# Which engine waits for the last store: SyncE's final semaphore wait placed on ScalarE

## The chip, the cores and the metric

One core of a Trainium2 chip. The metric is the device time of one execution in microseconds (us), median over the runs; every run also leaves its span, from its first to its last profiled instruction of the kernel. The device time is longer than the span, here by 1.4 us, and that difference is what this study is about. Where the timed interval starts no trace shows; where its end is placed among the trace's events below, it is counted from the span's start. All runs quoted are of the fast state. The one exception among the listed times is the first run of the kernel before, 324.55 us, which enters no comparison.

## The reference, cut to what matters

One decoding step: attention of one token over a window of 4096 cached keys (32 query heads, 16 key heads), and beside it a GELU layer, mixed by a gate. The result is a single row of 576 bfloat16 numbers.

```python
g = _sigmoid((x * gate_w).sum(-1, keepdims=True))
a = _A_ref(x, A_k_cache, A_v_cache, A_wq, A_wo)   # attention over the last 4096 positions
b = _B_ref(x, B_w1, B_b1, B_w2, B_b2)             # 576 -> 4608 -> 576 with GELU
return g * a + (1 - g) * b
```

Some 54 MB of cache and weights are read (53.62 MB by the page), 1152 bytes are written (one packet of the trace).

## The kernel before

The body ends with two casts of the accumulated row, one half on ScalarE and one on VectorE, and the store from SyncE's queue:

```python
    out_row = const.tile([1, D], BF16, name="out_row")
    nc.scalar.copy(out=out_row[:, DH:D], in_=y_out[1])
    nc.vector.tensor_copy(out=out_row[:, 0:DH], in_=y_out[0])
    nc.sync.dma_start(out=out.rearrange("a b d -> (a b) d"), in_=out_row[:])
```

When the program is complete, a function rewrites its closing block. Instead of one barrier that all engines pass, SyncE gets six event semaphores. Each waits until one semaphore has its final count and takes that count away again; the sixth is the store's own. GpSimd clears the other semaphores as two ranges as soon as ScalarE, TensorE and VectorE have drained (in the trace the last of the three drains, VectorE's, ends at 128.934 us, and the two clears run from 129.143 to 129.336).

```python
        sem = store.sync_info.on_update[0].id
        act = mybir.EngineType.Activation
        names = [i.name for i in end.instructions if i.engine == sp]
        names += [i.name for i in end.instructions if i.engine == act][1:]
        # ... mine: the waits on ScalarE's, VectorE's, two load queues' and TensorE's
        # ... semaphores, and last the store's
        for w, name in zip(mine, names):
            taken = mybir.SyncUpdate(..., update_mode="sem-sub-imm", update_value=w.wait_value)
            kept.append(copy.replace(leave, name=name,          # leave: an instruction of SyncE
                sync_info=mybir.SyncInfo(on_wait=[w], on_update=[taken])))
        for engine in (Activation, PE, DVE):                    # (cut) their drains
            kept.append(next(i for i in end.instructions if i.engine == engine))
        # ... GpSimd: wait for the three drains, two range clears
```

Of the kernel before, what the change touches and what calls it, by code (L numbers as in the profile page):

```python
# [18 lines left out]
def kernel(  # L19
# [91 lines left out]
    def store_ends_program(nc):  # L111
        body, end = nc.main_func.blocks[1], nc.main_func.blocks[2]
        sp, pool = mybir.EngineType.SP, mybir.EngineType.Pool
        store = [
            i
            for i in body.instructions
            if i.engine == sp and type(i).__name__ == "InstDMACopy"
        ][-1]
        sem = store.sync_info.on_update[0].id
        act = mybir.EngineType.Activation  # L120
        names = [i.name for i in end.instructions if i.engine == sp]
        names += [i.name for i in end.instructions if i.engine == act][1:]
        drain, arrive, leave = [i for i in end.instructions if i.engine == sp][:3]
        waits = list(drain.sync_info.on_wait)
        pe = [
            u
            for i in body.instructions
            if i.engine == mybir.EngineType.PE and i.sync_info
            for u in i.sync_info.on_update
        ]  # L130
        first = min(w.id for w in store.sync_info.on_wait)
        mine = [w for w in waits if w.id >= first and w.id != sem]
        mine.append(
            copy.replace(
                mine[0],
                id=pe[0].id,
                ant_name=pe[0].ant_name,
                wait_value=sum(u.update_value for u in pe),
            )
        )  # L140
        mine.append(next(w for w in waits if w.id == sem))
        stop = max(w.id for w in mine) + 1
        assert sorted(w.id for w in mine) == list(range(first, stop))
        waits = [w for w in waits if w.id < first]
        own = [i for i in body.instructions if i.engine == sp and i.sync_info]
        last_wait = max(
            n for n, i in enumerate(own) if any(w.id < first for w in i.sync_info.on_wait)
        )
        last_load = max(
            n for n, i in enumerate(own) if any(u.id < first for u in i.sync_info.on_update)  # L150
        )
        assert last_wait <= last_load
        assert len(names) >= len(mine)
        kept = []
        for w, name in zip(mine, names):
            taken = mybir.SyncUpdate(
                sync_type="semaphore",
                id=w.id,
                ant_name=w.ant_name,
                update_mode="sem-sub-imm",  # L160
                update_value=w.wait_value,
                update_reg=None,
            )
            kept.append(
                copy.replace(
                    leave,
                    name=name,
                    sync_info=mybir.SyncInfo(on_wait=[w], on_update=[taken]),
                )
            )  # L170
        for engine in (
            mybir.EngineType.Activation,
            mybir.EngineType.PE,
            mybir.EngineType.DVE,
        ):
            kept.append(next(i for i in end.instructions if i.engine == engine))
        ours = [i for i in end.instructions if i.engine == pool]
        others = mybir.SyncInfo(on_wait=waits, on_update=[])
        came = ours[1].sync_info
        three = mybir.SyncInfo(  # L180
            on_wait=[copy.replace(came.on_wait[0], wait_value=3)],
            on_update=[copy.replace(came.on_update[0], update_value=3)],
        )
        kept += [copy.replace(ours[0], sync_info=others), copy.replace(ours[1], sync_info=three)]
        reset, clear, spare, spare2 = ours[3:7]
        lo, hi = reset.reset_range_start, reset.reset_range_stop
        for n, (a, b) in enumerate(((lo, first), (stop, hi))):
            raw = list(clear.instr)
            assert raw[13:15] == [lo, hi - 1]
            raw[13:15] = [a, b - 1]  # L190
            words = dict(clear.ant_dict, range_first=a, range_last=b - 1)
            kept.append(
                copy.replace(
                    reset, name=(reset, spare)[n].name, reset_range_start=a, reset_range_stop=b
                )
            )
            kept.append(
                copy.replace(
                    clear, name=(clear, spare2)[n].name, instr=raw, ant_dict=words
                )  # L200
            )
        end.instructions = kept

    nc.at_finalize(store_ends_program)

    const = ctx.enter_context(tc.tile_pool(name="const", bufs=1))
# [561 lines left out]
```

## Time and profile before

| | kernel before |
|---|---|
| device time, three runs | 131.5, 131.64 us (and the 324.55 of the first run) |
| span of the profiled run, its device time | 130.1 us, 131.53 us |
| VectorE's last cast ends | 128.887 us |
| the store is issued, lands | 128.956, 130.079 us |
| SyncE's wait for it ends | 130.113 us |

Read it backwards from the end: the time beyond 130.11 is no instruction of the kernel, and between 129.24 and 130.08 no engine does anything that counts; one of them waits for the store. The prediction below shows the lines of the page on which this rests.

### The profile page before, as it was taken

The page shows a single profiled execution, that of the slowest core. Times are in us where ns is not written, and L with a number is a line of the kernel's source. Part 1 is how long each engine was busy: PE and PEld are TensorE (multiplying, and loading weights), DVE is VectorE, ACT ScalarE, POOL GpSimd, SP SyncE. Part 2 cuts the span into 40 slices and gives each one's busy share as a digit, 9 for nine tenths or more (in the row PEclk, how much of TensorE's full clock was granted, in tenths as well). Part 3 has the DMA queues.
Part 4 walks back from the last instruction along what each step waited for, and adds up shares of the span by engine and source line. Part 5 has one row for each costly group of instructions (what it writes and reads, how often), then busy time and mean ns, then how long its engine had stood idle before and what let it go on. Part 6 is the DMA issues. An engine that isn't in the chain of part 4 may idle for free.

```text
span 130.1 us, 2403 instructions
## 1 busy us (share of the span) xinstructions
PE 79.7 (61%) x1148; PEld 45.6 (35%) x1077; DVE 52.3 (40%) x48; ACT 8.3 (6%) x18; POOL 9.2 (7%) x26
## 2 busy tenths in 40 slices
PE   0037999476003998939918994995300830899573
PEld 0037679375000121201211120595300830855441
DVE  0153000400079959999999995614000020010001
ACT  2000000003000000030003003011000000000001
POOL 7039700000000000000000000000000000000000
PEclk9999999999999999999997799985555555559999
DMA  6999999799899999999899899899899899999980
GB/s 232 427 431 432 476 424 476 344 484 448 373 458 453 403 433 463 393 433 484 373 433 484 383 423 484 357 432 505 368 433 489 363 438 415 442 401 427 413 363 33
DMA packets 2508, 53.75 MB, mean 413 GB/s; under 512 B 286, under 2 KB 290, under 8 KB 580
## 3 DMA queue, kind: packets, MB, share of 16 engines
q1 hardware_dynamic: 2490, 53.61, 96.5%
q8 instruction: 8, 0.13, 0.4%
q10 hardware_dynamic: 10, 0.01, 0.0%
HBM read 53.62 MB, written 0.00 MB: 412 GB/s over the span
## 4 chain that ended last, share of the span: by engine, by line
DMA 52%; DVE 24%; PE 14%; issue 6%; SPq 2%
DMA k_t<-in_A_k_cache_dram 27%; DMA w_t<-in_B_w_dram 25%; DVE kt L531 19%; PE s_ps L553 7%; PE o_ps L640 5%; DVE m L569 3%; DVE pt L602 2%; PE y_ps L396 1%; SPq L684 1%; DVE mr L572 1%; SPq L691 0%; DVE out_row L736 0%; SPq L234 0%; SPq L230 0%; PE mt_ps L578 0%
## 5 line engine op out<-in xcount | busy, mean ns | idle before, releaser
L553 PE MATMUL s_ps<-kt,qz_flat 128*128 128x512 bf16 x128 | 32.9, 414 | 17.2 <-DVE kt L531 10.4
L531 DVE STREAM_TRANSPOSE kt<-k_t 128x4096 f32<-128x4096 f32 x8 | 35.3, 4433 | 12.2 <-DMA k_t<-in_A_k_cache_dram 10.5
L640 PE MATMUL o_ps<-pt,v_t 128*128 128x8 bf16 x512 | 14.2, 168 | 16.6 <-DMA v_t<-in_A_v_cache_dram 14.7
L553 PEld LDWEIGHTS <-qz_flat 128*128 128x128 bf16 x64 | 6.9, 107 | 40.6 <-issue 40.4
L640 PEld LDWEIGHTS <-v_t 128*128 128x128 bf16 x512 | 14.0, 102 | 17.3 <-DMA v_t<-in_A_v_cache_dram 14.9
L424 PEld LDWEIGHTS <-w_t 128*128 128x128 bf16 x162 | 10.3, 167 | 1.8 <-issue 1.8
L424 PE MATMUL h_ps<-x,w_t 128*128 128x2 bf16 x162 | 10.5, 202 | 0.0
L590 ACT ACTIVATE p_t<-s_ps,negm 128x1024 bf16<-128x1024 f32 x4 | 4.5, 1114 | 50.9 <-DVE negm L586 50.9
L396 PE MATMUL y_ps<-w_t,gt 128*1 128x288 bf16 x72 | 6.3, 329 | 1.2 <-DMA w_t<-in_B_w_dram 1.2
L670 DVE RECIPROCAL rg<-mt_ps 128x32 f32<-128x32 f32 x1 | 0.4, 358 | 15.6 <-PE mt_ps L665 15.6
L602 DVE STREAM_TRANSPOSE pt<-p_t 128x1024 bf16<-128x1024 bf16 x4 | 4.9, 1225 | 2.7 <-ACT p_t L590 2.7
L462 PE MATMUL q_ps<-x,wq_t 128*128 128x2 bf16 x144 | 4.0, 166 | 2.9 <-DMA wq_t<-in_A_wq_dram 2.9
L569 DVE TENSOR_REDUCE m<-s_ps 128x1 f32<-128x1024 f32 x4 | 4.8, 1196 | 1.1 <-PE s_ps L553 1.1
L396 PE MATMUL y_ps<-wo_t,ov 128*1 128x288 bf16 x62 | 4.3, 285 | 1.4 <-DMA wo_t<-in_A_wo_dram 1.4
L736 DVE CAST out_row<-y_ps 1x288 bf16<-1x288 f32 x1 | 0.4, 445 | 11.6 <-PE y_ps L396 11.6
L433 DVE COPY hacc<-h_ps 128x36 f32<-128x36 f32 x1 | 0.2, 196 | 11.9 <-PE h_ps L424 11.9
L462 PEld LDWEIGHTS <-wq_t 128*128 128x128 bf16 x144 | 3.9, 104 | 3.0 <-DMA wq_t<-in_A_wq_dram 3.0
L345 PE MATMUL xs_ps<-one_b,rows 1*128 1x1 bf16 x9 | 0.7, 196 | 6.9 <-DVE rows L339 6.9
L396 PEld LDWEIGHTS <-gt 128*1 128x1 bf16 x72 | 3.3, 92 | 3.4 <-issue 1.6
L694 DVE TENSOR_TENSOR om<-o_ps,rgh 128x128 bf16<-128x128 f32 x1 | 0.3, 291 | 8.6 <-PE o_ps L640 8.6
L396 PEld LDWEIGHTS <-ov 128*1 128x1 bf16 x62 | 2.6, 83 | 2.8 <-issue 1.9
L339 DVE COPY rows<-rows 1x1152 bf16<-1x1152 bf16 x1 | 0.7, 748 | 6.1 <-DMA rows<-in_A_x_dram 6.1
(72 smaller groups left out, 35.5 us busy)
## 6 DMA issues: line engine op xcount, KB each, us to landing
k_t<-in_A_k_cache_dram SPq DMA_DIRECT2D x4, 4096.0 KB, 32.1
v_t<-in_A_v_cache_dram SPq DMA_DIRECT2D x4, 4096.0 KB, 22.8
wq_t<-in_A_wq_dram SPq DMA_DIRECT2D x1, 4608.0 KB, 25.8
w_t<-in_B_w_dram SPq DMA_DIRECT2D x1, 2880.0 KB, 14.1
w_t<-in_B_w_dram SPq DMA_DIRECT2D x1, 2592.0 KB, 22.9
w_t<-in_B_w_dram SPq DMA_DIRECT2D x1, 2304.0 KB, 8.1
wo_t<-in_A_wo_dram SPq DMA_DIRECT2D x1, 2304.0 KB
wo_t<-in_A_wo_dram SPq DMA_DIRECT2D x1, 2160.0 KB
```

Source lines behind the costliest of these rows:

```text
L339: nc.vector.tensor_copy(out=xdup.rearrange("p (d t) -> p d t", t=2), in_=x_row.rearrange("p (d o) -> p d o", o=1).to_broadcast([1, D, 2]),)
L396: last = nc.tensor.matmul(y_out[s], lhsT=vec, rhs=row[:, s * DH : (s + 1) * DH], start=start, stop=stop, skip_group_check=True,)
L424: nc.tensor.matmul(h_ps[:, j:NF:NJ], lhsT=w1_t[:, i, j:FH:NJ], rhs=x2[:, i, :], start=False, stop=(i == NI - 1 and j == NJ - 1), skip_grou ...
L462: nc.tensor.matmul(q_ps[:, j : Hq : Hq // 2], lhsT=wq_t[:, i, j * Dh : (j + 1) * Dh], rhs=x2[:, i, :], start=(i == 0 and j == 0), stop=(i ...
L531: lambda: nc.vector.transpose(out=kt[g, f][:].bitcast(FP32), in_=keys.rearrange("p c d -> p (c d)").bitcast(FP32),),
L553: last = nc.tensor.matmul(s_ps[g][:, u * 512 : (u + 1) * 512].rearrange("p (c k) -> p c k", k=32), lhsT=qz(g, j, 2 * f + half), rhs=kv[:, ...
L569: queue("dve", lambda: nc.vector.reduce_max(out=m1[:], in_=s_ps[g][:], axis=AX.X))
L572: lambda: nc.vector.tensor_scalar(out=mr[:], in0=hi16[:], scalar1=m1[:, 0:1], scalar2=None, op0=ALU.mult),
L590: nc.scalar.activation(out=p_t[:].rearrange("p c k -> p (c k)"), in_=s_ps[g][:], func=ACT.Exp, bias=negm[:, 0:1], scale=SCALE, accum_out=s ...
L602: lambda: nc.vector.transpose(out=pt[:, g, :, :].rearrange("p c q -> p (c q)"), in_=p_t[:].rearrange("p c k -> p (c k)"),),
L640: last = nc.tensor.matmul(o_ps[:, 8 * g : 8 * g + 8, 0], lhsT=v_t[g][:, c, :], rhs=pt[:, g, c % 32, 8 * (c // 32) : 8 * (c // 32) + 8], st ...
L684: nc.sync.dma_start(out=wo_t[:, r0:r1, :].rearrange("p r n -> p (r n)"), in_=wo_src[:, 0 : 4 * RW, :].rearrange("h (a r) n -> h a (r n)", ...
```

## The change

The store's wait is moved from SyncE, which issued the store, to ScalarE, which has nothing else to do then (its last instruction, the drain, ends at 128.903). The intent is that SyncE gets through its five other take-backs and is finished early, and that an idle engine takes over the wait. The arithmetic, the loads and the store stay as they are. The two lines on `names` only lend the sixth take-back a spare name; it is taken off the list again (`kept.pop()`), and what it waits for goes to ScalarE's own closing instruction.

```diff
-        act = mybir.EngineType.Activation
         names = [i.name for i in end.instructions if i.engine == sp]
-        names += [i.name for i in end.instructions if i.engine == act][1:]
+        names.append([i.name for i in end.instructions if i.engine == pool][-1])
@@
+        landing = kept.pop().sync_info
         for engine in (Activation, PE, DVE):                    # (cut)
             kept.append(next(i for i in end.instructions if i.engine == engine))
+        event = [i for i in end.instructions if i.engine == mybir.EngineType.Activation][1]
+        kept.append(copy.replace(event, sync_info=landing))
```

## The prediction

Where the recorded text said more of the machine than a trace or a run of this case shows, it is cut, and the cut is marked. No term of its sum is among the cuts: 131.64 + 0.174 + 0.022 = 131.84 us if ScalarE is second in the order, 131.75 if it is fourth. Some of its words, in terms of the trace: a round, or the barrier, is nine updates of semaphore 2 in a row; "forward" are its first five updates, "the way back" its last four, "the turn" is the time from the fifth to the sixth; "the reset" are the writes to the semaphores 7 to 255 that the trace shows from 130.37 to 130.97. The records used here give an update's semaphore and its time and not its engine. The order of the engines is therefore the author's inference from when each one's last instruction ends, and e0 to e3 test it. That nothing afterwards absorbs the difference (step 5) is the author's estimate.

> **What bounds the kernel now.** I read the page from the front: the span, the slices, the chain that ended last; then the end of the program, because that is all that the change touches.
>
> ```profile
> span 130.1 us, 2403 instructions
> DMA  6999999799899999999899899899899899999980
> q1 hardware_dynamic: 2490, 53.61, 96.5%
> DMA 52%; DVE 24%; PE 14%; issue 6%; SPq 2%
> ```
>
> The transfers are busy in every slice but the last, and the queue of loads has 96.5% of the 16 engines' time. 53.6 MB have to be read, so loading is the bound, up to about 128 us. Nothing of that is in the diff: no load, no tile, no wait of the body changes. The chain in order of time shows what is left after the last load:
>
> ```profile
> 94.29 32.93 DMA w_t<-in_B_w_dram
> 127.22 0.04 issue
> 127.27 1.19 PE y_ps L396 x16
> 128.45 0.43 DVE out_row L736
> ```
>
> The last rows of w2 land at 127.2, sixteen matmuls and one cast follow, and the chain stops at 128.88. The timeline of the last two microseconds goes on:
>
> ```profile
> 128.44 0.45 DVE L736 CAST out_row<-y_ps 1x288 bf16<-1x288 f32 x1 [11.62 <-PE y_ps L396]
> 128.48 0.39 ACT L735 CAST out_row<-y_ps 1x288 bf16<-1x288 f32 x1 [11.47 <-PE y_ps L396]
> 128.96 0.28 SPq L737 DMA_DIRECT2D out_dram<-out_row  x1
> ```
>
> SyncE issues the store at 128.96. From there to the end of the span, 130.11, the page shows no busy engine. The view of the closing line of the program says what stands there:
>
> ```profile
> L763 SPq EVENT_SEMAPHORE  x6: 17/17/17, 129.3 to 130.1; - x6
> L763 POOLq EVENT_SEMAPHORE  x4: 17/30/43, 116.7 to 129.0; - x4
> L763 POOLq EVENT_SEMAPHORE_RANGE_CLEAR  x2: 33/52/71, 129.1 to 129.3; - x2
> L763 PEldq DRAIN  x1: 497/497/497, 128.0 to 128.0; - x1
> L763 ACTq DRAIN  x1: 421/421/421, 128.5 to 128.5; - x1
> ```
>
> SyncE's six semaphore instructions are what the diff is about: each waits for one semaphore and takes it back to zero. The columns give only count, duration and first and last start. The trace's own records, which the views merge, give each one (us from the span's start; semaphore 110 is the store's):
>
> ```
> SyncE event semaphores start   129.289 129.376 129.449 129.528 129.595 | 130.096 (on 110, ends 130.113)
> updates of semaphore 110       129.394   130.079   130.113
> last instruction ends          TensorE 128.525, ScalarE 128.903, VectorE 128.934, GpSimd 129.336
> updates of semaphore 2, after  128.731 129.062 129.863 129.907 130.250 | 130.294 130.333 130.367 130.413
> updates of semaphore 2, before -0.378 -0.344 -0.306 -0.262 -0.239 | -0.126 -0.088 -0.054 -0.007
> updates of semaphore 2, last   131.198 131.232 131.270 131.462 131.485 | 131.583 131.621 131.655 131.702
> ```
>
> Two things are to be seen. First, SyncE has done its five other take-backs at 129.61 and then stands until the store lands at 130.079; it wakes 17 ns later, and that is the last instruction of the span. Second, the program's end isn't the end of the time: 131.53 us were timed for this execution, 1.42 more than the span. No semaphore of the kernel is number 2; it goes up nine times in a row just before the first instruction, nine times after the last, and nine more times a microsecond later. Between the last two rows some 250 semaphores are written in five runs of numbers (7 to 53, 54 to 104, 105 to 155, 156 to 206, 207 to 255) from 130.37 to 130.97. So what follows the kernel waits for all engines, and the question of this change is only how late, and from which engine, that barrier is closed.
>
> [...] The trace shows these two updates of semaphore 110, at 129.394 and 130.079; only the second matters, whoever waits. [...]
>
> [...] Read the row "after". At 130.250 the fifth update comes, 137 ns after SyncE's last instruction. The four before it came at 129.907 or earlier, when SyncE still stood in its wait. So SyncE is fifth[...]. The first, at 128.731, can only be TensorE's, as all others were still in the program. The second, 129.062, is 159 ns after ScalarE's end (or 128 after VectorE's). The third, 129.863, comes after GpSimd's end at 129.336, and the fourth follows it by only 44 ns, so it belongs to an engine that was already waiting. I take the order TensorE, ScalarE, GpSimd, VectorE, SyncE. The trace leaves one alternative, ScalarE and VectorE exchanged.
>
> **The change part by part.** Removed from SyncE: its sixth event semaphore, which waited for 110. Added to ScalarE: the same instruction after its drain. Unchanged: the store, its landing, the five other take-backs, GpSimd's two range clears.
>
> 1. SyncE's five take-backs end at 129.61 before and after. They weren't on the path (0.47 us ahead of the landing), so SyncE gains nothing that counts: it goes into the barrier about 129.75 and stands there.
> 2. ScalarE ends its drain at 128.90, over a microsecond before the landing, so it is waiting at 130.079 as SyncE was. I give it the same 17 ns to wake and 17 to execute: 130.113. The span stays at 130.1.
> 3. From its last instruction to its barrier update ScalarE took 159 ns against SyncE's 137: plus 22 ns. ScalarE's update comes at about 130.272.
> 4. Before, when SyncE was the late one, the four others had already gone forward: only the way back was left, 130.250 to 130.413, or 163 ns. Now ScalarE is late, second in the row: GpSimd, VectorE and SyncE have still to go forward[...]. The round before the kernel has just that shape, as all came close together: second to ninth update, -0.344 to -0.007, 337 ns. It contains a turn of 113 ns (-0.239 to -0.126), where after the kernel the turn took 44[...].
> 5. Difference: 337 - 163 = 174, plus 22 of step 3, so about 0.20 us. It is the same at the sixth update[...]: 218 - 44 = 174. So nothing afterwards absorbs it.
>
> Sum: 131.64 + 0.20 = 131.84 us if ScalarE is second. If it is fourth, what remains is fourth to ninth, -0.262 to -0.007, 255 ns against 163: 92 + 22, so 0.11 us and 131.75. I weigh the first at four to one and say 131.8.
>
> **The rivals.** Rival one: the intent works and the end comes sooner, because SyncE is freed early and ScalarE answers faster. For it: SyncE is the last engine of the program. Against it: it is last only because of the landing, which waits for the DMA alone, 1.12 us from the start of its issue. The wake was 17 ns, so there is nothing to be saved there; even an instant one gives 131.62. Rival two: nothing at all, because the timed interval stops before the barrier or because the reset work of an engine released early hides it. For it: I can't see where the timed interval starts and stops. Against it: 1.42 us lie outside the span, about what the barrier and the reset take[...]. It would make 131.64. Rival three: ScalarE does something more before the barrier than its 159 ns, as GpSimd does (129.336 to 129.863, 0.53 us). Then plus 0.5: 132.1 to 132.2. Against it: ScalarE's own 159 ns in the same trace. Rival four: the instructions reach ScalarE late, or the loads shift. There is no sign of it; the body keeps its order.
>
> **Range and chances.** All rivals lie between 131.6 and 132.2; two quiet runs before were 131.5 and 131.64, so noise of 0.15 is added below. Range 131.5 to 132.2. Two per cent is 2.6 us, more than the whole stretch from the store's issue to the span's end (1.15 us) and more than any rival: within 2% at 97 in 100. The rest is for a different chip state, a little more on the slow side, since the granted clock fell to five tenths in nine slices of before.
>
> **What would show it.** Right: the span stays within 0.2 us of 130.1 with its last event semaphore on ScalarE some 17 ns after the store's landing; SyncE's list has five instead of six and ends near 129.6; semaphore 2 has only one update (TensorE's) ahead of that moment, then eight in a chain of about 0.34 us. Step 4 is wrong if three or four updates are already there (ScalarE then stands late in the order), step 3 if ScalarE's update comes much later than 0.16 us after its last instruction, and step 5 if the chain is longer and the time isn't. The whole prediction falls if the landing itself moves by more than 0.3 us against the store's issue, or if the time changes in the body, ahead of 128.

## The result, and the profile after

| | before | changed |
|---|---|---|
| median of the first comparison | 131.63 us (4 runs) | 131.84 us (131.66 to 132.01, 4 runs) |
| ratio, 95% interval | | 1.0019 [0.9999, 1.0039] |
| span of the profiled run | 130.1 us | 130.3 us |
| device time less span, profiled run | 1.42 us | 1.59 us |

A ratio is the mean time of one kernel's fast runs over that of the other's of the same rounds, so not quite the ratio of the medians quoted. The interval touches 1, so from these runs' times alone one couldn't say that anything happened. The trace says it.

The page's first lines of the changed kernel, with the queue of loads as busy as before:

```profile
span 130.3 us, 2403 instructions
q1 hardware_dynamic: 2490, 53.61, 96.4%
```

The closing line of the program in the changed kernel (the columns are count, shortest, median and longest duration in ns, first and last start):

```profile
L765 SPq EVENT_SEMAPHORE  x5: 17/17/17, 129.4 to 129.8; - x5
L765 POOLq EVENT_SEMAPHORE  x4: 17/30/43, 116.8 to 129.1; - x4
L765 POOLq EVENT_SEMAPHORE_RANGE_CLEAR  x2: 33/52/71, 129.3 to 129.5; - x2
L765 ACTq DRAIN  x1: 419/419/419, 128.6 to 128.6; - x1
L765 ACTq EVENT_SEMAPHORE  x1: 17/17/17, 130.3 to 130.3; - x1
```

SyncE has five instead of six and is done at 129.8. The sixth stands on ScalarE, 1.2 us after its drain, and starts at 130.3 as SyncE's started at 130.1. Where the 0.2 us between these two come from, the timeline of the end shows:

```profile
128.61 0.45 DVE L738 CAST out_row<-y_ps 1x288 bf16<-1x288 f32 x1 [11.65 <-PE y_ps L398]
128.64 0.39 ACT L737 CAST out_row<-y_ps 1x288 bf16<-1x288 f32 x1 [11.49 <-PE y_ps L398]
129.12 0.28 SPq L739 DMA_DIRECT2D out_dram<-out_row  x1
```

The casts start 0.16 us later in this run than in the one of before (128.44 there), and the store likewise. That lies ahead of everything that was changed, and the chain in order of time puts it with the loads, whose last rows land at 127.39 in place of 127.22:

```profile
127.39 0.04 issue
127.43 1.19 PE y_ps L398 x16
128.62 0.43 DVE out_row L738
```

It is a difference of these two runs and not of the kernels: over all runs the spans' median is 130.25 us for the changed kernel here and 130.30 in a later set, and 130.3 to 130.4 for the kernel before in three later sets. What is left is after the store. The trace's records, in us from the span's start:

```
                                         before                            changed
store lands (semaphore 110)              130.079                           130.243
event semaphore on 110, end              130.113 (SyncE)                   130.281 (ScalarE)
semaphore 2, first round after           128.731 129.062 129.863 129.907   128.895
                                         130.250                           130.430 130.469 130.513 130.536
                                         130.294 130.333 130.367 130.413   130.634 130.672 130.706 130.753
landing to ninth update                  0.334                             0.510
last round, fourth and ninth update      131.462 131.702                   131.799 132.040
device time                              131.53                            131.87
```

Before, four updates were there when the landing came, and five followed it. In the changed kernel only TensorE's is there, and eight follow in a chain of 0.32 us. From the landing on, the changed kernel takes 0.176 us more up to the ninth update, and 0.174 more up to the last one of the last round (1.797 against 1.623). The device time ends 0.17 us ahead of that last update in both. So the two profiled runs' 0.34 us are 0.164 up to the landing, by chance, and 0.176 in the barrier after it.

### The profile page after: what moved, and what is told of

It is laid out like the page before. It is cut to its first block, busy times and chain, and to the rows that moved or that the text cites. A ratio compares the mean times of both kernels' runs of the same rounds, so it can differ in the third digit from the quotient of the medians.

```text
span 130.3 us, 2403 instructions
## 1 busy us (share of the span) xinstructions
PE 80.8 (62%) x1148; PEld 45.7 (35%) x1077; DVE 52.3 (40%) x48; ACT 8.3 (6%) x18; POOL 9.2 (7%) x26
## 3 DMA queue, kind: packets, MB, share of 16 engines
q1 hardware_dynamic: 2490, 53.61, 96.4%
## 4 chain that ended last, share of the span: by engine, by line
DMA 50%; DVE 24%; PE 15%; issue 6%; SPq 3%
DMA k_t<-in_A_k_cache_dram 27%; DMA w_t<-in_B_w_dram 23%; DVE kt L533 19%; PE s_ps L555 9%; PE o_ps L642 5%; DVE m L571 3%; DVE pt L604 2%; SPq L686 2%; PE y_ps L398 1%; DVE mr L574 1%; SPq L693 0%; SPq L236 0%; DVE out_row L738 0%; SPq L232 0%; PE mt_ps L580 0%
## 5 line engine op out<-in xcount | busy, mean ns | idle before, releaser
L398 PE MATMUL y_ps<-w_t,gt 128*1 128x288 bf16 x72 | 6.9, 343 | 1.2 <-DMA w_t<-in_B_w_dram 1.2
```

Source lines behind the costliest of these rows:

```text
L398: last = nc.tensor.matmul(y_out[s], lhsT=vec, rhs=row[:, s * DH : (s + 1) * DH], start=start, stop=stop, skip_group_check=True,)
```

## The experiments

As in the prediction, "the barrier" is the round of nine updates of semaphore 2; the "place theory" is the prediction's account, that each engine's first update has a fixed place in that round and that the cost is set by the place of the late engine, which e0 to e3 test; "landing to ninth" is the time from the store's landing to the ninth update of the first round after the kernel. "Outside the span" is the device time less the span, median over the runs of a set. For the kernel before it is 1.44, 1.43 and 1.41 us in three sets (11, 11 and 9 runs), steadier than the device time, in which the body's 0.1 to 0.2 us are contained. Three calls were made; the four kernels of each ran on one chip against shared runs of the kernel before.

### First call: the wait on each of the other engines

**e0, ScalarE again.** The changed kernel, no edit, more rounds.

> The changed kernel as it is, with more rounds, since one set of four runs left the interval at 0.9999 to 1.0039. Place theory[...]: +0.18 us against before, ratio about 1.0014, and in the trace 0.51 us from the store's landing to the ninth update of semaphore 2 (before 0.33). Rival, the body: the 0.16 us that the changed kernel's profile showed ahead of the store is real; then +0.35 us, ratio 1.0027, with the store issued 0.16 us later than before again. Rival, nothing: 1.0000.

Measured: ratio 1.0015 [0.9999, 1.0032], 131.93 against 131.70 us. Landing to ninth 0.510 us again; outside the span 1.64 us against 1.44. The profiled run's store is issued late again, at 129.185 against 128.956, as the rival "body" expected; but the spans have the same median, 130.3, and the profiled runs of e6 and e7, which have the body of the kernel before, issue it at 129.224 and 129.065. So that rival is out. The size agrees with the place theory; the interval of the times still touches 1, and the evidence is the trace and the time outside the span: all ten runs of the changed kernel have 1.56 to 1.65 us there, 29 of the 31 of the kernel before 1.39 to 1.48.

**e1, VectorE.**

```diff
-        event = [i for i in end.instructions if i.engine == mybir.EngineType.Activation][1]
+        event = [i for i in end.instructions if i.engine == mybir.EngineType.DVE][1]
```

> The landing wait on VectorE. Place theory with the order TensorE, ScalarE, GpSimd, VectorE, SyncE: VectorE's update is the fourth, after three that are there already; fourth to ninth takes 0.25 us as before the kernel, so landing to ninth is about 0.43 us if VectorE needs as long as ScalarE from its last instruction to its update (0.15), +0.10 us, ratio 1.0008. If VectorE and ScalarE were exchanged in the order, its update is second and the cost +0.18. Rival, ScalarE itself answers slowly or does more at its end and the place is irrelevant: as before, 0.33 us, ratio 1.0000.

Measured: ratio 1.0020 [1.0001, 1.0039], landing to ninth 0.485 us. Three updates are there before the landing (128.834, 129.162, 129.958), and VectorE's is the fourth, 130.424. So VectorE is fourth, ScalarE second, and the one alternative that the prediction left open is excluded. Fourth to ninth took 0.240 us (expected 0.25). VectorE needed 0.196 us from its last instruction to its update, more than the 0.15 assumed. The time outside the span, 1.77 us, is 0.2 more than this chain makes of it; see e10.

**e2, TensorE.** The same edit with `PE`.

> The landing wait on TensorE. Place theory: TensorE is first, so no update of semaphore 2 comes before its own, and the whole round of nine follows, 0.36 us; TensorE took 0.245 us from its last instruction to its update. Landing to ninth 0.64 to 0.68 us, +0.30 to +0.35 us against before, ratio 1.0023 to 1.0027; the largest but for GpSimd. Rival, ScalarE alone is slow: as before. Rival, any engine but SyncE costs the same: +0.18.

Measured: ratio 1.0030 [1.0012, 1.0049]. No update comes before 130.752, then nine in 0.357 us. Landing to ninth 0.705 us, a little over the expected 0.68, of which 0.269 are TensorE's way from its last instruction to its update (0.245 expected) and 0.051 the event semaphore itself, which takes 17 ns on the others and 21 on VectorE:

```profile
L765 SPq EVENT_SEMAPHORE  x5: 17/17/17, 129.6 to 129.9; - x5
L765 PEldq EVENT_SEMAPHORE  x1: 51/51/51, 130.4 to 130.4; - x1
```

In this view of e2's closing line SyncE is again done half a microsecond ahead of the landing, which is at 130.404. Outside the span are 1.72 us against 1.44, and 0.045 more lie inside it, as the event semaphore ends 79 ns after the landing instead of 34: together some 0.33 of the trace's 0.371.

**e3, GpSimd.** The wait comes after its range clears.

```diff
-        event = [i for i in end.instructions if i.engine == mybir.EngineType.Activation][1]
-        kept.append(copy.replace(event, sync_info=landing))
@@ after the range clears
+        kept.append(copy.replace(ours[1], name=ours[-1].name, sync_info=landing))
```

> The landing wait on GpSimd, after its two range clears. Place theory: GpSimd is third, two updates are there, third to ninth takes about 0.29 us. GpSimd took 0.53 us from its last instruction to its update before; [...]landing to ninth is 0.85 us, +0.52 us against before, ratio 1.0040. If the 0.53 us are the range clear still at work, which the landing then hides, it is 0.17 us instead and the cost +0.15 us. Rival, ScalarE alone is slow: as before.

Measured: ratio 1.0051 [1.0027, 1.0075]; landing to ninth 0.882 us, two updates ahead of the landing; outside the span 2.00 us against 1.44, so 0.56 more where the trace has 0.548. From GpSimd's last instruction to its update 0.557 us pass, though the last range clear had ended 0.79 us before that instruction did. So this half microsecond isn't the clears at work; what GpSimd does in it no record shows.

The four late engines and SyncE side by side (us, from the traces; the way home is from the late engine's update to the ninth):

| late engine | place | updates ahead of the landing | last instruction to its update | way home | landing to ninth |
|---|---|---|---|---|---|
| SyncE (before) | 5 | 4 | 0.137 | 0.163 | 0.334 |
| VectorE (e1) | 4 | 3 | 0.196 | 0.240 | 0.485 |
| GpSimd (e3) | 3 | 2 | 0.557 | 0.284 | 0.882 |
| ScalarE (e0) | 2 | 1 | 0.150 | 0.322 | 0.510 |
| TensorE (e2) | 1 | 0 | 0.269 | 0.357 | 0.705 |

The way home grows with each place towards the front, step by step by 77, 44, 38 and 35 ns. The rival "ScalarE alone is slow" would have left e1, e2 and e3 at 0.33 us. ScalarE's own way out is next to the shortest.

### Second call: no landing to wait for, and a different store

**e4 and e5, an early store.** Their outputs are wrong, which doesn't matter for the times. Both store a row that VectorE makes early, e4 in the kernel before and e5 in the changed one. The lowest semaphore of the take-backs is then named by VectorE's, as the store no longer waits for it.

```diff
+    b2_early = const.tile([1, D], BF16, name="b2_early")
+    nc.vector.tensor_copy(out=b2_early[:], in_=b2g[:])
@@
-        first = min(w.id for w in store.sync_info.on_wait)
+        first = min(w.id for w in waits if w.ant_name.startswith('DVE'))
@@
-    nc.sync.dma_start(out=out.rearrange("a b d -> (a b) d"), in_=out_row[:])
+    nc.sync.dma_start(out=out.rearrange("a b d -> (a b) d"), in_=b2_early[:])
```

> Wrong result on purpose: the kernel before, but the store carries a row that VectorE makes early (the scaled b2), so it lands before the last cast ends and the landing wait on SyncE is met at once. Place theory: the late engine of the barrier is then GpSimd (0.53 us after its last instruction), third in the order; third to ninth takes 0.28 us. Ninth update about 1.26 us after VectorE's last cast ends, where before it was 1.53: the time falls by some 0.27 us, ratio 0.998. Rival, the time is set by something else than the landing: no change.

> Wrong result on purpose: the changed kernel with the same early store. Place theory: a wait that ends early costs nothing wherever it stands, because GpSimd is late in both, so this agrees with e4_early_syncE within 0.02 us in the trace (cast end to ninth update 1.26 us) and within noise in time. Rival, the instruction on ScalarE, or ScalarE's end of program, costs the 0.18 us by itself: then this is 0.18 us slower than e4_early_syncE and close to before.

Measured: the store is issued at 101.74 and 101.96 us, among the loads, and lands at 128.29 and 128.09, ahead of the last cast's end (129.10 and 129.13). Cast end to ninth update is 1.253 and 1.252 us, as expected (1.26), and equal in the two. But the times hardly fell: ratios 0.9996 [0.9979, 1.0012] and 0.9999 [0.9987, 1.0011] where 0.998 was expected. The barrier gained its 0.27 us and the end lost most of them: in e5's trace the cast's end to the end of the device time is 2.562 us against 2.643 before. (e4's profiled run, 132.16 us, is the slowest of its set and lost more, 3.057.) What the traces show there: in both, a packet of 8192 bytes appears at 131.46 and 131.48 us, on the queue that also brings packets of that size before the kernel starts (six of them, from -11.32 to -8.60 us, in the trace of before, where they are of the kind "instruction"), lasting 0.995 and 0.493 us; the writes to the semaphores 156 to 206, called VectorE's resets here because e10 moves them, start at 130.79 and 130.82 in place of 130.43, although the ninth update came earlier (130.35 and 130.38, by the cast's end and the time after it, against 130.413); and the device time follows the end of that packet, less 0.29 us, in both. The kernel before and the changed one have no such packet. e1 has one, at 131.757. Common to e1, e4 and e5 is one instruction more on VectorE: 59 recorded in the trace, 58 in the kernel before and in the changed one. I took the packet for instructions of VectorE, which was a guess (the expectations call the packet a fetch, and the guess the fetch theory).

**e6 and e7, the store in pieces.** The kernel before, the store described as 2 by 288 (e6) and 16 by 36 (e7).

```diff
-    nc.sync.dma_start(out=out.rearrange("a b d -> (a b) d"), in_=out_row[:])
+    nc.sync.dma_start(out=out.rearrange("a b (h d) -> (a b) h d", h=2), in_=out_row[:].rearrange("p (h d) -> p h d", h=2))
```

> The kernel before (wait on SyncE) with the store described as 2 pieces of 288 in place of one of 576, to see whether the landing can come sooner. I have no firm number: 1.12 us from issue to landing as before, give or take 0.1. Place theory: whatever is gained at the landing is gained at the ninth update one for one, up to the 0.27 us at which GpSimd becomes the late engine; what is lost is lost in full.

> The same with 16 pieces of 36. [...] Issue to landing 1.0 to 1.3 us; the ninth update follows the landing by 0.33 us as before, as SyncE is the late engine still, unless the landing gains more than 0.27 us.

Measured: ratios 0.9999 [0.9985, 1.0014] and 1.0002 [0.9990, 1.0014]; issue to landing 1.123 and 1.128 us; landing to ninth 0.334 in both. These runs test nothing about stores. Each trace has one packet of 1152 bytes, as before, and the instructions of both, compared engine by engine with those of before, are the same: the split of contiguous data was folded together when the program was built. What they give is a control: the same end of program, run twice more, is 0.334 us to the nanosecond, and outside the span 1.43 us both times. Whether the landing can be had sooner stays untried.

### Third call: the early store without the added instruction, and that instruction alone

**e8 and e9, a store of zeros.** Their outputs are wrong, which doesn't matter for the times. As e4 and e5, but the row stored is a part of a tile that is zero anyway, so no engine's instructions are more.

```diff
-    nc.sync.dma_start(out=out.rearrange("a b d -> (a b) d"), in_=out_row[:])
+    nc.sync.dma_start(out=out.rearrange("a b d -> (a b) d"), in_=zeros[64:65, NZ : NZ + D])
```

> Wrong result on purpose: the kernel before with the store carrying zeros that lie ready, so no instruction is added on any engine (the first pair of early stores put one more on VectorE[...]). Place theory: GpSimd is the late engine, cast end to ninth update 1.25 us as in the first pair; with no fetch the timed end follows the ninth by 1.12 us as before, so the time falls by 0.27 us, ratio 0.998. Rival, the first pair's lack of gain was not the fetch: no change in time again, ratio 0.9996.

> Wrong result on purpose: the changed kernel with the same store of zeros. Place theory: the same as e8_early_zero_syncE within noise (cast end to ninth update 1.25 us, ratio 0.998), as the landing wait is met at once and GpSimd is late in both. Rival, the instruction on ScalarE costs by itself: 0.18 us above e8_early_zero_syncE.

Measured: ratios 0.9968 [0.9956, 0.9981] and 0.9970 [0.9956, 0.9983]. No packet at the end. Cast end to ninth 1.254 us in both (1.526 before), cast end to the end of the device time 2.385 and 2.377 us (2.643 before): 0.26 us less, as the place theory has it, with the wait on SyncE and with the wait on ScalarE alike. ScalarE's instruction is there in e9 and passes at once:

```profile
L765 SPq EVENT_SEMAPHORE  x5: 17/17/17, 129.0 to 129.3; - x5
L765 ACTq EVENT_SEMAPHORE  x1: 17/17/17, 129.0 to 129.0; - x1
```

In this view of e9's closing line ScalarE's event semaphore starts at 129.0, right behind its drain, and the late engine is GpSimd (update at 129.93, then 0.284 us home). The medians fell by more than the traces' 0.26 us, by 0.40 and 0.42; the spans, which are given to 0.1 us, place the rest, about 0.1 us, ahead of the last cast in both kernels. Its cause isn't known; the store among the loads (issued at 101.8, landed at 128.2 in e8) is one more thing that differs in these runs.

**e10, the instruction alone.** The kernel before, wait on SyncE, with the additional copy of e4 and nothing else.

```diff
+    b2_early = const.tile([1, D], BF16, name="b2_early")
+    nc.vector.tensor_copy(out=b2_early[:], in_=b2g[:])
```

> The kernel before with one more small VectorE copy early on, off the path; wait on SyncE. Fetch theory: [...]a packet of 8192 bytes of instructions appears at the end of the trace, VectorE's run of semaphore resets (156 to 206) starts some 0.35 us later, and the time outside the span grows from 1.43 to about 1.63 us, ratio 1.0015, although no wait has moved. Rival, that packet belongs to the event semaphore on VectorE in e1_dve and to the early stores: no packet, 1.43 us.

Measured: the packet of 8192 bytes is there, at 131.656 us for 0.474 us; VectorE's resets start at 131.00, 0.55 us after the sixth update (130.446), where before they started 0.14 after it (130.429 after 130.294); outside the span 1.52 us against 1.41; ratio 1.0004 [0.9991, 1.0016]. So the packet comes with VectorE's one more instruction, here with the wait on SyncE as in e4, and in e5 with the wait on ScalarE. Its cost is 0.1 us here by the medians, half of what I expected, and the ratio alone would not show it; from the landing to the device time the profiled run has 1.608 us against 1.451 before, 0.16 more. In e1 it is 0.21 (1.811 against 1.451, less the 0.151 of its chain), and e1's packet is 0.048 us longer. How the packet costs this isn't shown: VectorE's resets start 0.66 us before the packet does, so its transfer isn't what holds them back, and that both belong to a fetch of VectorE's last instructions, no trace shows. The page shows the copy in its counts, and nothing of the packet, which comes after the span:

```profile
span 130.3 us, 2404 instructions
PE 81.0 (62%) x1148; PEld 46.3 (36%) x1077; DVE 52.5 (40%) x49; ACT 8.3 (6%) x18; POOL 9.4 (7%) x26
```

In these two lines of e10's page VectorE (DVE) has 49 busy instructions, where before it had 48, and 2404 in all against 2403.

**e11, VectorE at the old length.** The wait on VectorE as in e1, with one copy moved away.

```diff
-    nc.vector.tensor_copy(out=hacc[:], in_=h_ps[:])
+    nc.scalar.copy(out=hacc[:], in_=h_ps[:])
```

> The landing wait on VectorE as in e1_dve, with one copy of its body (hacc) given to ScalarE, so VectorE's stream is as long as before. Place theory with the fetch taken out: landing to ninth update 0.485 us as in e1_dve (+0.15), no packet of instructions at the end, time outside the span 1.57 us in place of the 1.77 of e1_dve, ratio 1.0012. Rival, the wait on VectorE itself makes the longer tail: 1.77 us again.

Measured: landing to ninth 0.485 us, exactly e1's. But the packet is there again, at 131.932, and outside the span are 1.72 us, not 1.57; ratio 1.0017 [1.0004, 1.0030]. The edit missed its aim: the trace counts 59 instructions on VectorE, one copy less but one event semaphore more than e1 (10 in place of 9), as hacc now comes from ScalarE. So this run doesn't refute the fetch theory, and doesn't measure the wait on VectorE without it either. In all fourteen traces it is the same: where VectorE has 58 instructions there is no packet (before, changed, e0, e2, e3, e6 to e9), where it has 59 there is one (e1, e4, e5, e10, e11).

### A version that beats both

None came out. SyncE, the engine of the kernel before, is the best place for the wait of all five (landing to ninth 0.334 us against 0.485 to 0.882). e8 shows that another 0.26 us lie in an earlier landing, at which GpSimd becomes the late engine; no correct kernel here has it.

## Why the prediction was right

**What bounds the kernel.** Right: the body is untouched. The queue of loads has 96.4% after 96.5%, and the spans have the same median within 0.1 us over the later sets. The 0.16 us that the first pair of profiles shows in the body didn't repeat.

**Step 1, the five take-backs.** Right: they end at 129.77, 0.47 us before the landing, and were 0.47 us ahead of it in the kernel before. SyncE is freed early for nothing: the fifth update, its own, comes only at 130.536.

**Step 2, the wake.** Right: ScalarE's event semaphore starts 21 ns after the landing, SyncE's started 17 after it, and takes the same 17 ns.

**Step 3, ScalarE's way to its update.** Right in kind, 149 ns in place of 159, so 12 more than SyncE instead of 22.

**Step 4, the way home.** Right: 323 ns in place of 337, against SyncE's 163. The 14 ns are those of the turn (fifth to sixth update), within one: 98 ns where the round before the kernel, the pattern taken, had 113. e0 to e3 show the way home for every place but SyncE's, and e1 settles the order that the prediction gave four to one.

**Step 5, nothing absorbs it.** Right: from the ninth update to the last one it is 1.287 us after 1.289. The sum, 0.196 us expected, is 0.176 in the trace and 0.15 to 0.20 by the time outside the span (1.59 and 1.64 us against 1.44); 131.84 was worked out for this order, and 131.84 is the median measured. That the two agree to the last digit is luck, since runs of one kernel differ by some tenths. Two smaller readings are wrong or loose and change no sum: TensorE's last instruction ends at 128.486 in the trace, not 128.525, and the first of the nine updates "after the last" instruction comes at 128.731, ahead of it.

**The rivals.** That the end would come sooner falls with the trace: ScalarE wakes no faster than SyncE (21 ns against 17), and the ninth update follows the landing 0.176 us later. That the instruction on ScalarE costs by itself falls with e8 and e9, which agree. That it would cost nothing falls with the time outside the span, 1.59 and 1.64 us against 1.44. That ScalarE would do something more on its way out falls with its 0.15 us; GpSimd is the engine that does (0.56 us, e3).

**What stays open.** What exactly ends the device time. It lies 0.17 to 0.18 us before the last update of the last round in eight of the nine profiled runs without the packet, 0.29 us before the packet's end in the five with one, and 0.04 us before that last update in e3, which neither rule explains (e3's profiled run has 2.10 us outside the span, where four of the other five have 1.98 to 2.02). Two runs of the kernel before, of 31, have 0.5 to 0.6 us more outside the span (132.31 and 132.24 us), and what happened in them no profile shows; e2, e3 and e4 have one such run each (2.29, 2.54 and 2.56 us), of which e4's is the profiled one, with a packet of 0.995 us where the four others took 0.474 to 0.522.

## What to carry to other kernels

In these traces the wait at the end of the program is not over when it is met: from the landing to the ninth update 0.334 us pass with the wait on SyncE, whose update is the fifth, and 0.485 to 0.882 with it on one of the four engines whose update comes ahead of SyncE's (e0 to e3). From the late engine's own update to the ninth it is 0.163 us for SyncE and 0.240 to 0.357 for the four, so here the engine that finishes last had best be SyncE. Whether the order is the same in another program these runs don't show; look it up in that program's trace. Work taken from an engine that is waiting anyway gained nothing (SyncE's five take-backs end 0.47 us ahead of the landing in both kernels). For differences of a tenth of a microsecond compare the traces from a common event on (here the landing) and the time outside the span, and count each engine's instructions, because an experiment that adds a single one can add a packet of instructions at the end (e10: 8192 bytes, and 1.52 us outside the span against 1.41).
